# Reordering the first tile of a retention and maxout kernel: table load, decay tables, state steps, weight conversion and weight sums

## The chip, the cores and the metric

The kernel runs on one core of a Trainium2 chip. A core has a matrix engine (TensorE, PE in the profile, with its weight loads listed apart as PEld), a vector engine (VectorE, DVE), an activation engine (ScalarE, ACT), a general engine (GpSimd, POOL) and an engine that here only starts transfers (SyncE, SP). Each has its own queue of instructions and they wait for each other by semaphores. Data lies in a large on-chip memory (SBUF), and matrix products land in accumulators (PSUM). The metric is the time of one execution on the device, in microseconds (us), as the median of several runs.

## What is computed

Two steps follow each other. The first is a retention block (attention with a fixed decay in place of a softmax) over 8 batches, 8 heads, 576 positions and a head size of 64. The second is a feed-forward block: the larger of three products with three weight matrices, times a fourth.

```python
scores = scale * np.matmul(q, k.transpose(0, 1, 3, 2))
gamma = 1.0 - 2.0 ** (-5.0 - np.arange(H, dtype=np.float32))
Dmat = np.where(rel >= 0, gamma[:, None, None] ** rel[None, :, :], 0.0)   # rel: query minus key position
ret = scores * Dmat[None, :, :, :]
attn = np.matmul(ret, v).astype(np.float32)
x = attn.transpose(0, 2, 1, 3).reshape(B * S, H * D)                      # 4608 x 512
h = np.maximum(np.maximum(x @ w1, x @ w2), x @ w3)                        # 4608 x 768
return (h @ w_out).astype(np.float32)                                     # 4608 x 512
```

q, k and v are float32. The four weight matrices are float64 numbers, given to the kernel as 64-bit integers. The kernel makes float32 weights out of their bits.

## The kernel before

**Chunks and tiles.** The 4608 rows are cut into 36 chunks of 128 rows for retention and 9 tiles of 512 rows (four chunks) for the feed-forward block. While tile t goes through the feed-forward block, the chunks of tile t + 1 go through retention, step by step between the products; `steps` (L633) lists which step comes where. The chunks of tile 0 come first, alone, written out by hand at L603 to L631. There is no scheduler: every engine runs its instructions in the order in which the program text issues them.

**Retention of a chunk g.** `load(g)` (L151) starts the transfers of k, q and v, and the queue of SyncE also carries the weights. `decay_values` (L159) multiplies v by the key decay gk on GpSimd. `transposes` (L167) turns k and q on PE, and ScalarE copies the result out (L181). `scores` (L183) multiplies them on PE (L189), and VectorE masks the result into `st` (L192). `state` (L201) multiplies keys and decayed values (L208) into what is carried to the next chunk, and `keep` (L211) finishes it on VectorE (L216, or L218 and then GpSimd's L219) with the state decay gs. `values` (L227) makes the output: `st` times values (L241), and the carried state times q (L253); VectorE multiplies it by the output decay gq into `xT` (L260), the input of the feed-forward block. So the state of a chunk must be ready before the L253 products of the next.

**Conversion of the weights.** A piece is a block of 128 by 512 weights; there are 24: 18 of the three matrices and 6 of the fourth (`out`). `convert_all` (L418) is a generator that makes a piece in four steps, so that they can be laid between other work: `convert(n)` runs n steps. Of a piece, VectorE has five instructions: exponent bits (L428), fraction bits (L433), whole mantissa (L439), sign and exponent (L444) and the product (L450); ScalarE has three (L429, L431, L434). After a piece's product the load of the piece six further on is started (`load_weights(1)`), into one of the six buffers of the pool `wraw`.

**The feed-forward block of tile 0.** `ffn(0)` runs nine units of two products each. A unit (fp, i) covers matrix i and the blocks 2fp and 2fp + 1 of the hidden vector h. `up_plain` (L551) makes a product on PE in one of four accumulators, which are used in turn (two of the pool `ps_x`, two of `ps_y`). For the first matrix ScalarE copies it into h (L558), for the others VectorE takes the maximum (L557). Between the product and its maximum stands a call of `convert`, so that on VectorE the conversion steps lie ahead of the maximum in its queue. After the nine units `downs_plain` (L538) multiplies h with the fourth matrix: six rounds of four matmuls, into the same four accumulators (L543), so that the first four matmuls need the last four products out of these.

**Tiles 1 to 8** use Strassen's scheme (seven products of half size in place of eight; `up` and `downs`). For this the weights need sums and differences of their quarters: `weight_sums(n)` (L463) makes them for unit n with two instructions on VectorE (L471, L472) and two on GpSimd (L473, L474). Their tiles come from a pool `late`, which takes the memory of the conversion's buffers once `while_converting` is closed. Before, the first three units' sums come at the last three rounds of the down product, and the other six are put on a list of chores, which `up` works off at three places of each unit of tile 1 (`chore`), two in the first two places and none in the third. In `up`, the last product (product 3) adds to the accumulator x after VectorE has read it (L522).

**Transfers at the start.** ScalarE's queue starts the decay tables: gk (L100), gs (L599, two) and gq (L602, four). Its first copy (L181) is preceded by a load of the activation table; in the profile it stands between these transfers and the first copy.

Of the kernel before, what the change touches and what calls it, by code (L numbers as in the profile page):

```python
# [34 lines left out]
FP32 = mybir.dt.float32  # L35
# [16 lines left out]
def kernel(  # L52
# [14 lines left out]
    nc = tc.nc  # L67
    P = 128
# [3 lines left out]
    NP = H // 2  # L72
    NG = B * S // C
    NDC = DM // P
    NF = DF // P
# [22 lines left out]
    gq = const.tile([P, NP, C], FP32, name="gq")  # L98
    gs = const.tile([P, NP, D], FP32, name="gs")
    nc.scalar.dma_start(gk[:], key_decay)  # L100

    ident = const.tile([P, P], FP32, name="ident")
    make_identity(nc, ident[:])
# [47 lines left out]
    def load(g):  # L151
        if g >= BY_PE and ("q", g) not in raws:
            load_blocks(g, *range(C // 32))
        for n, src in (("k", k), ("q", q), ("v", v)) if g < BY_PE else (("k", k), ("v", v)):
            t = raws[n, g] = raw.tile([C, H, D], FP32, tag=n, name=n + "raw", bufs=4 if n == "k" else 3)
            for row, b, pos, m in spans(g):
                nc.sync.dma_start(t[row:row + m], src[b, :, pos:pos + m, :].rearrange("h p d -> p h d"))
# [37 lines left out]
    def begins(g):  # L195
        return g + 1 < NG and start_of(g + 1) != 0

    def half(j):
        return slice(D * j, D * (j + 1))

    def state(g):  # L201

        kr = raws["k", g]
        if begins(g):
            r = start_of(g) or 0
            kvs[g] = ps_r.tile([P, NP, D], FP32, tag="r", name="kv")
            for h in range(H):
                nc.tensor.matmul(kvs[g][half(h % 2), h // 2, :], lhsT=kr[r:, h, :], rhs=vds[g][r:, h, :],  # L208
                                 start=True, stop=True)

    def keep(g):  # L211
        if begins(g):
            kv = kvs.pop(g)
            t = states[g + 1] = stp.tile([P, NP, D], FP32, tag="state", name="state")
            if start_of(g) is not None:
                nc.vector.tensor_tensor(t[:], kv[:], gs[:], op=ALU.mult)  # L216
            else:
                nc.vector.tensor_tensor(t[:], kv[:], states[g][:], op=ALU.add)  # L218
                nc.gpsimd.tensor_tensor(t[:], t[:], gs[:], op=ALU.mult)  # L219
# [7 lines left out]
    def values(chunks, new_states=()):  # L227

        def before(g):
            return C if start_of(g) is None else start_of(g)

        t, i = divmod(chunks[0], CPT)
        pool, tag = (ps_r, "r") if chunks[0] >= CPT - 1 else (ps_y, "y")
        o = [pool.tile([P, len(chunks), NP // 2, C], FP32, tag=tag, name="o") for _ in range(2)]
        for m, g in enumerate(chunks):
            for n in range(NP):
                for c in range(2):
                    h = head(c, n)  # L240
                    nc.tensor.matmul(o[n % 2][half(c), m, n // 2, :], lhsT=vds[g][:, h, :],  # L241
                                     rhs=sts[g][:, h % 2, h // 2, :], start=m == 0 and n < 2,
                                     stop=before(g) == 0, skip_group_check=True)
        for g in new_states:
            state(g)
        for m, g in enumerate(chunks):
            old = before(g)
            if old > 0:
                for n in range(NP):
                    for c in range(2):  # L250
                        h = head(c, n)
                        r = half(h % 2)
                        nc.tensor.matmul(o[n % 2][half(c), m, n // 2, :old], lhsT=states[g][r, h // 2, :],  # L253
                                         rhs=qks[g]["q"][r, h // 2, :old], start=False, stop=True,
                                         skip_group_check=True)
        if i == 0:
            xT[t] = xpool.tile([P, NDC, NT], FP32, tag="xT", name="xT")
        for b in range(2):
            shape = [P, NP // 2, len(chunks), C]
            nc.vector.tensor_tensor(  # L260
                xT[t][:, b::2, i * C:(i + len(chunks)) * C].rearrange("p u (m c) -> p u m c", c=C),
                o[b][:].rearrange("p m u c -> p u m c"), gq[:, b::2, :].unsqueeze(2).to_broadcast(shape), op=ALU.mult)
        for g in new_states[:1]:
            keep(g)
        i += len(chunks) - 1
        if i == CPT - 1 and t > 0:
            x = xT[t]
            a11, a12, a21, a22 = (x[:, 2 * d:2 * d + 2, NH * r:NH * (r + 1)] for r in range(2) for d in range(2))
            s1, s2, s3, s4 = (spool.tile([P, 2, NH], FP32, tag=f"S{n}", name=f"S{n}") for n in (1, 2, 3, 4))
            nc.vector.tensor_tensor(s1[:], a21, a22, op=ALU.add)  # L270
            nc.vector.tensor_tensor(s2[:], s1[:], a11, op=ALU.subtract)
            nc.gpsimd.tensor_tensor(s3[:], a11, a21, op=ALU.subtract)
            nc.gpsimd.tensor_tensor(s4[:], a12, s2[:], op=ALU.subtract)
            xS[t] = {1: a11, 2: a12, 3: s4[:], 4: a22, 5: s1[:], 6: s2[:], 7: s3[:]}
# [4 lines left out]

    one = const.tile([P, 1], FP32, name="one")
    nc.vector.memset(one[:], 1.0)
    top = const.tile([P, 1], FP32, name="top")
    nc.vector.memset(top[:], 1151.0 * 2.0 ** 23)
    inf = const.tile([P, 1], FP32, name="inf")
# [176 lines left out]
    def weight_sums(n):  # L463
        if n >= len(units):
            return
        fp, i = units[n]
        half = [slice(0, DM // 2), slice(DM // 2, DM)]
        b11, b21 = (w_sb[i, 2 * fp][:, r] for r in half)
        b12, b22 = (w_sb[i, 2 * fp + 1][:, r] for r in half)
        t1, t2, t4 = (late["pool"].tile([P, DM // 2], FP32, name=f"T{m}_{i}_{fp}")[:] for m in (1, 2, 4))  # L470
        nc.vector.tensor_tensor(t1, b12, b11, op=ALU.subtract)  # L471
        nc.vector.tensor_tensor(t2, b22, t1, op=ALU.subtract)  # L472
        nc.gpsimd.tensor_tensor(b12, b22, b12, op=ALU.subtract)  # L473
        nc.gpsimd.tensor_tensor(t4, b21, t2, op=ALU.subtract)  # L474
        wT[fp, i] = {1: b11, 2: b21, 3: b22, 4: t4, 5: t1, 6: t2, 7: b12}
# [3 lines left out]
    def convert(n):  # L479
        for _ in range(n):  # L480
            next(converting, None)
# [78 lines left out]
    def ffn(t):  # L560

        h = hpool.tile([P, NF, NT], FP32, tag="h", name="h")
        for n, (fp, i) in enumerate(units):
            if t == 0:
                for fb in (2 * fp, 2 * fp + 1):
                    maximum = up_plain(t, h, fb, i)
                    convert(4)
                    maximum()
            else:
                if t == 1 and n == 0:  # L570
                    sums_of_outs()
                for _ in up(t, h, fp, i):
                    pass
                if i == 2:
                    sums_of_hidden(h, fp)
            yield
        if t == 0:
            convert(6)
            for fb, _ in enumerate(downs_plain(t, h)):
                convert(4 if fb < 2 else 4 * len(pieces))  # L580
                if fb in (1, 3):
                    yield
                if fb == 3:
                    while_converting.close()
                    late["pool"] = ctx.enter_context(tc.tile_pool(name="late", bufs=1))
                if fb > 2:
                    weight_sums(fb - 3)
            for n in range(3, len(units), 2):
                chores.extend([partial(weight_sums, n), partial(weight_sums, n + 1), lambda: None])
        else:  # L590
            chore(len(chores))
            for n, _ in enumerate(downs(t, h)):
                if n in (1, 3):
                    yield
        yield


    for j in range(2):
        nc.scalar.dma_start(gs[half(j)], state_decay[half(j), :, half(j)])  # L599
    for c in range(2):  # L600
        for b in range(2):
            nc.scalar.dma_start(gq[half(c), b::2, :], out_decay[half(b ^ c), NP // 2 * c:NP // 2 * (c + 1), :])  # L602
    warm(6)  # L603
    for g in range(CPT):
        load(g)
    load_weights(2)
    load(CPT)
    load_weights(4)
    decay_values(0)
    transposes(0)  # L610
    warm(2)
    scores(0)
    transposes(1)
    decay_values(1)
    values([0], [0])
    scores(1)
    transposes(2)
    decay_values(2)
    values([1], [1])
    transposes(3)  # L620
    decay_values(3)
    scores(2)
    convert(2)
    scores(3)
    convert(4)
    values([2], [2])
    decay_values(4)
    convert(2)
    values([3], [3])
    transposes(4)  # L630
    convert(2)  # L631

    def steps(t):  # L633

# [92 lines left out]
```

## Time and profile before

The time before is 799.95 us (median of 3 runs, 799.31 to 800.62); the profiled execution has a span of 797.8 us.

| stretch, us | what it holds | PE busy, us | DVE busy, us |
|---|---|---|---|
| 0 to 10 | first loads, chunk 0 | 6.84 | 0.30 |
| 10 to 20 | chunks 0 to 2 | 10.00 | 4.85 |
| 20 to 30 | chunks 2 and 3, first weights | 6.90 | 9.93 |
| 30 to 120 | tile 0, chunks 4 to 7 | 90.0 | 77.5 |
| 120 to 140 | end of tile 0, start of tile 1 | 18.70 | 17.79 |
| 140 to 700 | tiles 1 to 7 | 560.0 | 271.2 |
| 700 to 798 | tile 8 | 94.89 | 33.57 |

In the profile, the share of a stage is worth more than the share of the span: DVE is busy for 52% of the span but for 86% of the time from 30 to 120 us. A row of a timeline gives the start, the length, the engine, the line, the operation with its tiles and shapes, and in brackets the idle time ahead of it with what ended it. The table load of ScalarE takes 1.28 us and starts at 5.29; the first copy of kT starts at 6.58, that of qT at 7.07, and the first scores at 7.71. The first weight piece is waited for by ScalarE until 20.67. The nine units run from 30.16 to 103.9, the down product from 103.78 to 128, with retention between its rounds; conversion ends at 115.8. Weight sums run on VectorE and GpSimd from 124.4 to 149.5.

### The profile page before, as it was taken

The page shows a single profiled execution, that of the slowest core. Times are in us where ns is not written, and L with a number is a line of the kernel's source. Part 1 is how long each engine was busy: PE and PEld are TensorE (multiplying, and loading weights), DVE is VectorE, ACT ScalarE, POOL GpSimd, SP SyncE. Part 2 cuts the span into 40 slices and gives each one's busy share as a digit, 9 for nine tenths or more (in the row PEclk, how much of TensorE's full clock was granted, in tenths as well). Part 3 has the DMA queues.
Part 4 walks back from the last instruction along what each step waited for, and adds up shares of the span by engine and source line. Part 5 has one row for each costly group of instructions (what it writes and reads, how often), then busy time and mean ns, then how long its engine had stood idle before and what let it go on. Part 6 is the DMA issues. An engine that isn't in the chain of part 4 may idle for free.

```text
span 797.8 us, 13706 instructions
## 1 busy us (share of the span) xinstructions
PE 787.3 (99%) x5128; PEld 645.1 (81%) x5128; DVE 415.1 (52%) x833; ACT 174.0 (22%) x401; POOL 139.7 (18%) x158
## 2 busy tenths in 40 slices
PE   8899999999999999999999999999999999999998
PEld 7545546888888888888888888888888888888887
DVE  2897978664354634463535344543546344632341
ACT  2654642111111102111111111111111121112211
POOL 2110107421210130112211121112111201110000
PEclk9999999999999999999999999999999999999999
DMA  9985543333333332432233333333333323001001
GB/s 221 232 219 125 154 108 100 58 56 57 87 57 57 57 73 53 77 58 61 60 55 57 66 83 57 56 56 91 56 55 58 81 55 66 1 14 40 1 1 53
DMA packets 237506, 59.27 MB, mean 74 GB/s; under 512 B 218240, under 2 KB 236160, under 8 KB 237440
## 3 DMA queue, kind: packets, MB, share of 16 engines
q1 hardware_dynamic: 236176, 58.01, 33.2%
q8 instruction: 40, 0.66, 0.4%
q10 hardware_dynamic: 1264, 0.40, 0.2%
q14 instruction: 26, 0.21, 0.1%
HBM read 48.89 MB, written 9.44 MB: 73 GB/s over the span
## 4 chain that ended last, share of the span: by engine, by line
PE 96%; issue 1%; ACTq 1%; ACT 1%; DMA 0%; SPq 0%; POOL 0%; DVE 0%; DVEq 0%; POOLq 0%
PE x L492 31%; PE z L492 15%; PE dx L364 11%; PE up L554 8%; PE y L492 8%; PE dz L364 5%; PE s L189 4%; PE o L241 4%; PE dy L364 3%; PE down L543 2%; PE o L253 2%; PE kv L208 2%; PE kt L179 0%; PE qt L179 0%; ACTq L602 0%
## 5 line engine op out<-in xcount | busy, mean ns | idle before, releaser
L492 PE MATMUL x<-S,T 128*128 128x256 f32 x576 | 148.0, 379 | 0.2 <-ACT p L497 0.2
L492 PEld LDWEIGHTS x<-S,T 128*128 128x128 f32 x576 | 109.0, 190 | 16.0 <-ACT p L497 0.6
L342 POOL TENSOR_TENSOR H<-h 128x256 f32<-128x256 f32 x24 | 20.9, 872 | 320.8 <-DVE h L535 320.8
L492 PE MATMUL x<-xT,w 128*128 128x256 f32 x288 | 76.1, 387 | 0.0
L492 PE MATMUL x<-S,w 128*128 128x256 f32 x288 | 74.4, 381 | 1.1 <-DVE h L522 1.1
L492 PE MATMUL y<-xT,w 128*128 128x256 f32 x288 | 73.9, 379 | 0.0
L492 PE MATMUL z<-xT,T 128*128 128x256 f32 x288 | 73.9, 379 | 0.0
L492 PE MATMUL z<-S,w 128*128 128x256 f32 x288 | 73.9, 379 | 0.0
L522 DVE TENSOR_TENSOR tmp<-x,p 128x256 f32<-128x256 f32 x48 | 20.4, 425 | 100.0 <-PE x L492 100.0
L497 ACT COPY p<-x 128x256 f32<-128x256 f32 x72 | 26.8, 372 | 192.1 <-PE x L492 192.0
L260 DVE TENSOR_TENSOR xT<-o,gq 128x512 f32<-128x512 f32 (+1 forms) x40 | 23.6, 632 | 85.9 <-PE o L253 84.6
L554 PE MATMUL up<-xT,w 128*128 128x512 f32 x144 | 64.2, 601 | 0.0
L492 PEld LDWEIGHTS x<-S,w 128*128 128x128 f32 x288 | 49.3, 189 | 14.6 <-DVE h L522 1.5
L492 PEld LDWEIGHTS y<-xT,w 128*128 128x128 f32 x288 | 54.7, 190 | 7.4
L492 PEld LDWEIGHTS z<-S,w 128*128 128x128 f32 x288 | 54.7, 190 | 7.4
L492 PEld LDWEIGHTS x<-xT,w 128*128 128x128 f32 x288 | 53.0, 190 | 9.6 <-issue 1.5
L492 PEld LDWEIGHTS z<-xT,T 128*128 128x128 f32 x288 | 54.3, 189 | 7.9
L554 PEld LDWEIGHTS up<-xT,w 128*128 128x128 f32 x144 | 27.1, 193 | 32.2 <-issue 29.3
L219 POOL TENSOR_TENSOR state<-state,gs 128x256 f32<-128x256 f32 x24 | 19.8, 825 | 188.3 <-DVE state L218 188.3
L192 DVE TENSOR_TENSOR st<-s,causal 128x512 f32<-128x512 f32 x72 | 45.0, 684 | 13.8 <-PE s L189 12.9
L497 ACT COPY u<-x 128x256 f32<-128x256 f32 x72 | 26.8, 372 | 100.1 <-PE x L492 90.3
L161 POOL TENSOR_TENSOR vd<-vraw,gk 128x512 f32<-128x512 f32 x36 | 38.7, 1075 | 56.1 <-DMA vraw<-in_v_dram 56.1
(92 smaller groups left out, 1089.3 us busy)
## 6 DMA issues: line engine op xcount, KB each, us to landing
out_dram<-osb SPq DMA_DIRECT2D x35, 256.0 KB, 2.1
kraw<-in_k_dram SPq DMA_DIRECT2D x32, 256.0 KB, 3.0
vraw<-in_v_dram SPq DMA_DIRECT2D x32, 256.0 KB, 3.5
qraw<-in_q_dram SPq DMA_DIRECT2D x464, 16.0 KB, 1.8
kxraw<-in_k_dram SPq DMA_DIRECT2D x464, 16.0 KB, 1.8
bits<-in_moe_w_dram SPq DMA_DIRECT2D x18, 256.0 KB, 4.4
bits<-in_moe_w_dram SPq DMA_DIRECT2D x36, 128.0 KB, 4.1
bits<-in_moe_w_out_dram SPq DMA_DIRECT2D x6, 512.0 KB, 4.9
```

What stands on the lines that cost most here:

```text
L161: nc.gpsimd.tensor_tensor(t[:], raws.pop(("v", g))[:], gk[:].unsqueeze(2).to_broadcast([C, H, D]), op=ALU.mult)
L189: nc.tensor.matmul(s[j][:, p, :], lhsT=kT[r, p, :], rhs=qT[r, p, :], start=True, stop=True)
L192: nc.vector.tensor_tensor(st[:, j], s[j][:], masks[start_of(g)][:].unsqueeze(1).to_broadcast([C, NP, C]), op=ALU.mult)
L219: nc.gpsimd.tensor_tensor(t[:], t[:], gs[:], op=ALU.mult)
L241: nc.tensor.matmul(o[n % 2][half(c), m, n // 2, :], lhsT=vds[g][:, h, :], rhs=sts[g][:, h % 2, h // 2, :], start=m == 0 and n < 2, stop=be ...
L260: nc.vector.tensor_tensor(xT[t][:, b::2, i * C:(i + len(chunks)) * C].rearrange("p u (m c) -> p u m c", c=C), o[b][:].rearrange("p m u c - ...
L342: chores.append(lambda: (pool(s3, a11, a21, op=ALU.subtract), pool(s4, a12, s2, op=ALU.subtract)))
L364: nc.tensor.matmul(out[m], lhsT=hS[n](fp)[:, m * P:(m + 1) * P], rhs=late["T"][n][:, fp, :], start=first and fp == 0 and (m == 0 or last a ...
L492: nc.tensor.matmul(out[:], lhsT=w[:, d * P:(d + 1) * P], rhs=xS[t][n][:, d, :], start=first and d == 0, stop=d == 1, skip_group_check=True)
L497: nc.scalar.copy(c[:], src[:])
L522: nc.vector.tensor_tensor(c22, x[:], p7[:], op=ALU.add)
L554: nc.tensor.matmul(ps[:], lhsT=w_sb[i, fb][:, dc * P:(dc + 1) * P], rhs=xT[t][:, dc, :], start=(dc == 0), stop=(dc == NDC - 1))
```

## The change

It has five parts.

1. ScalarE copies one number (`first`) ahead of everything else, so that its table is loaded at the start and not in front of the first kT.
2. The state decay is loaded by SyncE behind the loads of chunk 1, and the output decay by ScalarE behind the copies of chunk 0's q and k, so that chunks 0 and 1 come ahead of them.
3. In the first four chunks the `state` and `keep` steps are called by themselves and earlier: `state` ahead of `values`, and `keep` ahead of the conversion steps that it stood behind. The call of `convert(4)` between `scores(3)` and the values is split and put behind.
4. In the last six of the nine units `convert` runs five steps a product in place of four, so that conversion is finished before the down product.
5. The sums of six units, not three, are then called in the six rounds of the down product, and the other three are spread over the chores one by one.

```diff
@@ tables
     nc.scalar.dma_start(gk[:], key_decay)
+    one = const.tile([P, 1], FP32, name="one")
+    nc.vector.memset(one[:], 1.0)
+    first = const.tile([P, 1], FP32, name="first")
+    nc.scalar.copy(first[:], one[:])
@@ state(g), keep(g)
         kr = raws["k", g]
+        kvs[g] = None
...
+        kv = kvs[g]
         if begins(g):
-            kv = kvs.pop(g)
@@ values
         for g in new_states:
-            state(g)
+            if g not in kvs:
+                state(g)
...
         for g in new_states[:1]:
-            keep(g)
+            if g >= CPT:
+                keep(g)
@@ ffn
                     maximum = up_plain(t, h, fb, i)
-                    convert(4)
+                    convert(4 if fp == 0 else 5)
                     maximum()
...
-            convert(6)
+            convert(4 * len(pieces))
+            while_converting.close()
+            late["pool"] = ctx.enter_context(tc.tile_pool(name="late", bufs=1))
             for fb, _ in enumerate(downs_plain(t, h)):
-                convert(4 if fb < 2 else 4 * len(pieces))
+                weight_sums(fb)
                 if fb in (1, 3):
                     yield
-                if fb == 3:
-                    while_converting.close()
-                    late["pool"] = ctx.enter_context(tc.tile_pool(name="late", bufs=1))
-                if fb > 2:
-                    weight_sums(fb - 3)
-            for n in range(3, len(units), 2):
-                chores.extend([partial(weight_sums, n), partial(weight_sums, n + 1), lambda: None])
+            for n in range(NF, len(units)):
+                chores.extend([partial(weight_sums, n), lambda: None, lambda: None])
@@ the first chunks
-    for j in range(2):
-        nc.scalar.dma_start(gs[half(j)], state_decay[half(j), :, half(j)])
-    for c in range(2):
-        for b in range(2):
-            nc.scalar.dma_start(gq[half(c), b::2, :], out_decay[half(b ^ c), NP // 2 * c:NP // 2 * (c + 1), :])
     for g in range(CPT):
         load(g)
+        if g == 1:
+            for j in range(2):
+                nc.sync.dma_start(gs[half(j)], state_decay[half(j), :, half(j)])
...
     transposes(0)
+    for c in range(2):
+        for b in range(2):
+            nc.scalar.dma_start(gq[half(c), b::2, :], out_decay[half(b ^ c), NP // 2 * c:NP // 2 * (c + 1), :])
     warm(2)
     scores(0)
     transposes(1)
     decay_values(1)
+    state(0)
     values([0], [0])
+    keep(0)
     scores(1)
     transposes(2)
     decay_values(2)
+    state(1)
+    keep(1)
     values([1], [1])
...
     scores(2)
     convert(2)
     scores(3)
+    state(2)
+    keep(2)
+    convert(2)
+    values([2], [2])
+    convert(2)
+    decay_values(4)
+    values([3], [3])
+    keep(3)
+    transposes(4)
     convert(4)
-    values([2], [2])
-    decay_values(4)
-    convert(2)
-    values([3], [3])
-    transposes(4)
-    convert(2)
```

More of the change, by code (lines that the diff above doesn't have):

```diff
@@ L274, in values @@
             xS[t] = {1: a11, 2: a12, 3: s4[:], 4: a22, 5: s1[:], 6: s2[:], 7: s3[:]}
-    one = const.tile([P, 1], FP32, name="one")
-    nc.vector.memset(one[:], 1.0)
     top = const.tile([P, 1], FP32, name="top")
```

## The prediction

> **What bounds the kernel now.** I read the busy shares first, then where TensorE (PE) waits, then the clock in those stretches, then VectorE's (DVE's) own order. The page's first line says that nothing but PE is near its limit over the whole span:
>
> ```profile
> PE 787.3 (99%) x5128; PEld 645.1 (81%) x5128; DVE 415.1 (52%) x833; ACT 174.0 (22%) x401; POOL 139.7 (18%) x158
> ```
>
> Only 10.5 us of 797.8 are idle on PE, so any gain must come from the few places where it waits. PE's timeline (start, length, idle before it and what ended that) names the two that matter here:
>
> ```profile
> 27.74 0.67 PE L253 MATMUL o<-qT,state 64*64 64x128 f32 x16 [3.01 <-POOL state L219]
> ...
> 30.16 7.87 PE L554 MATMUL up<-xT,w 128*128 128x512 f32 x16
> ...
> 134.88 1.13 PE L492 MATMUL x<-S,w 128*128 128x256 f32 x4 [1.08 <-DVE h L522]
> ```
>
> Windows of 3.41 us cut at the clock's steps (length; PE, PEld, DVE, ACT, POOL busy; granted clock) show what a wait costs beyond its length: where PE was busy for 0.56 of 3.41 us, and also for 1.69, the next 3.41 us ran at 0.50:
>
> ```profile
> 24.89:28.30 3.41, 0.56 (x16) 0.43 (x16) 3.38 (x8) 1.44 (x2) 1.72 (x2) 1.00 0.85 229
> 28.30:31.71 3.41, 3.41 (x14) 2.40 (x11) 3.41 (x6) 1.95 (x4) 1.67 (x2) 0.50 0.94 233
> 4.43:7.84 3.41, 1.69 (x14) 1.25 (x14) 0.00 (x0) 2.36 (x3) 0.68 (x1) 1.00 1.05 242
> 7.84:11.25 3.41, 3.41 (x24) 3.15 (x24) 1.29 (x2) 0.45 (x1) 0.50 (x2) 0.50 0.97 221
> ```
>
> DVE's timeline from 20 us on shows who holds the first product back: it works without a gap from 19.75 to 36 us, and xT of chunk 3, the last input of the first up product (L554 at 30.16), is at its end:
>
> ```profile
> 20.95 0.42 DVE L428 TENSOR_SCALAR expo<-bits 128x512 int32<-128x512 int32 x1
> ...
> 26.09 0.41 DVE L218 TENSOR_TENSOR state<-kv,state 128x256 f32<-128x256 f32 x1
> 26.42 0.68 DVE L439 SCALAR_TENSOR_TENSOR mant<-frac,mant 128x512 f32<-128x512 int32 x1
> 27.02 1.21 DVE L444 SCALAR_TENSOR_TENSOR expo<-bits,expo 128x512 int32<-128x512 int32 x1
> 28.27 1.42 DVE L450 TENSOR_TENSOR w<-mant,expo 128x512 f32<-128x512 f32 x1
> 29.60 0.74 DVE L260 TENSOR_TENSOR xT<-o,gq 128x256 f32<-128x256 f32 x2
> ```
>
> Last, DVE late in tile 0: xT of chunks 4 and 5 comes after a wait, the last maximum at 104.43, and between the two DVE has 0.28 us to spare out of 31.85:
>
> ```profile
> 73.26 1.29 DVE L260 TENSOR_TENSOR xT<-o,gq 128x512 f32<-128x512 f32 x2 [2.97 <-PE o L253]
> ...
> 104.43 0.68 DVE L557 TENSOR_TENSOR h<-h,up 128x512 f32<-128x512 f32 x1
> ...
> 73.26:105.11 31.85, 31.85 (x108) 15.38 (x109) 31.57 (x57) 17.31 (x27) 3.05 (x3) 1.00 0.63 170
> ```
>
> [...] in the timeline the maximum at 104.43 indeed stands behind conversion steps. [...] L444 and L450 took 1.21 and 1.42 us beside GpSimd's 26.58 to 29.13, 0.69 elsewhere.
>
> **The change, part by part.**
>
> *Table load and decay tables.* The load (1.28 us, from 5.29) leaves qT's path: qt ends at 5.98, so scores(0) can start near 6.2, not 7.71: 1.5 us earlier. 384 KB of tables leave the head of the transfers but are still sent before chunk 3. The transfers run at 200 to 280 GB/s from 2 us on, so chunk 3's q (landed 17.6) and the first weight piece (landed 20.6, which ScalarE's L429 waited for at 20.67) come about as before, 0.5 us earlier at best. ScalarE's FIFO now holds kT of chunk 1 behind four table issues (0.63 each, one waiting for chunk 1's v, near 9 us), and DVE's xT of chunk 0 waits for these tables until some 12.5 us, with state and scores(1) behind it. Both end before the 17.6 us of chunk 3's q. So I pay nothing for it and gain nothing by itself.
>
> *States ahead of weights.* DVE's order before xT of chunk 3 was: first piece, its second piece whole, states. In the built program after the change it is: two steps of piece one (0.67), scores 3 (1.20), state (0.33), the rest of piece one (1.93), xT of chunk 2 (0.67), two steps of piece two (0.67), xT of chunk 3 (0.67): 6.1, plus 0.5 where GpSimd's L219 collides (L433 took 0.95 at 30.93 beside it). From 20.65 that ends at 27.3; with the weights 0.5 earlier, 26.8. The 3.01 us wait goes (state at 22.85, L219 0.85, PE at 23.8). First up product: from 30.2 to 27.1 (the middle of 26.8 and 27.3), **3.1 earlier**. Its second half needs the second piece, which DVE now ends 3.5 later (state, three steps, two collisions), when PE gets there; the next unit needs pieces two and three at 34 to 36, and PE is there at 36. Its clock decides the rest. PE is idle for some 1.7 us before it, and 0.25 before qt of chunk 4. Before, this product lay partly in the cold window and lost 0.75 (7.8 against 7.0 to 7.1 later). Warm, it gains these: 3.9. Wholly cold it loses 1.7 against 0.75: 2.2. A window that holds both waits is 43% busy, under the 50% that was enough at 7.84, so cold is a little likelier; I take **2.6** for the step, ends 2.0 and 4.2.
>
> *Five steps a product.* A piece is four steps and 2.60 us of DVE (0.335+0.335+0.60+0.72+0.61, start to start). From xT of chunks 4 and 5 to the last maximum stand eight products. With eight more steps, ten pieces stand there and not eight: 5.2 us more on an engine with 0.28 to spare. The other work is the same (6 maxima of 0.60, 4 scores, 2 transposes, 2 states, xT, GpSimd collisions 1.85): 36.9 us and not 31.8. Queued behind the converted pieces is that maximum, and behind it PE: L543's fourth matmul uses the accumulator that the last up product filled. PE wants it at 103.88 + 3 × 0.86 = 106.45, that is 33.2 us after xT; before, the maximum ended at 105.11 and left 1.3 to spare. Now it ends 37.0 us after: a **stall of 3.8** (0.75 at the third matmul, the rest at the fourth). It doesn't depend on how early the stage begins: DVE reaches xT at about 67.5 and waits for PE there, as it did for 2.97. Such a gap leaves some window under 50% busy however it falls, so the clock halves for 3.41 us, of which 1.2 to 1.7 is lost: **1.5**. Ends for both together: 3.3 (no halving, collisions 0.5 less) and 6.5 (a collision of vd with DVE, 0.85, more).
>
> *Six sums in tile 0.* Four pairs (eight sums on DVE) now lie in the 5.3 us in which DVE waited for PE before 121.11, plus what ends conversion earlier; contended, 4 × 1.8 = 7.2, from about 108 to 115, so hidden. Between xT and the first h of tile 1, DVE has two pairs fewer, contended 1.4 to 1.8 each. L522, at 134.42, moves ahead of PE's need: the 1.08 wait goes. **1.1 gained**, ends 0 and 1.3.
>
> Sum: 2.6 − 3.8 − 1.5 + 1.1 = **1.6 slower**: 799.95 + 1.6 = 801.6.
>
> **Rivals.** *No change:* the first product starts warm (3.9), or the stall costs no clock. 3.9 − 3.8 − 1.5 + 1.1 = 0.3 slower; with no halving 1.2 faster: about 800. For it: half-busy windows[...]. Against: PE's 1.7 us gap at the first product. *Faster:* DVE's extra 5.2 us find slack and no maximum is waited for. Then 3.0 + 1.1 come through: 795.8. For it: DVE is 52% busy overall, waits 2.97 at 73.26, and conversion ended at 115.74, 5 us ahead of its use at 121. Against: none of this slack lies between xT and the last maximum. *Much slower:* cold first product (2.0), stall 4.6 with another collision, 1.7 of clock, 0.8 back: 3.5 slower, 803.5.
>
> **How the numbers follow.** Forecast 0.42, no change 0.31, faster 0.13, much slower 0.14. The forecast lies at the bound of 0.2% (1.6 us): 0.32 of it falls to slower, 0.10 to within. No change gives 0.29 within and 0.02 slower. So faster 0.13, same 0.39, slower 0.48. The range 798.8 to 803.6 leaves out the faster case and the outer part of the last.
>
> **What would show it.** Right: no wait at L253 near 24; first up product at 26.8 to 27.4; a wait of PE at the third and fourth matmul of the down product, ended by DVE's maximum, 3 to 4 us in all; a clock of 0.50 after it; no wait at the first tile-1 product 3. Wrong: DVE idle between xT of chunks 4, 5 and the last maximum, a down product that starts without a wait, or first weights landing well before 20.

## The result and the profile after

The changed kernel takes 809.48 us (median of 5 runs, 808.57 to 811.34) against 799.95: a ratio of 1.0117, interval 1.0098 to 1.0136, 9.5 us slower. The direction was forecast, the size was not (1.6; upper end of the range 803.6).

The page's first line says little again. PE's busy time rose by 2.9 us with the same number of instructions, and the span by 10.0 (807.8 against 797.8):

```profile
PE 790.2 (98%) x5128; PEld 645.0 (80%) x5128; DVE 413.2 (51%) x833; ACT 174.4 (22%) x402; POOL 139.8 (17%) x158
```

The down product and the first product of tile 1 on PE before, from the start of the one to the start of the other without a wait:

```profile
103.78 13.90 PE L543 MATMUL down<-w_out,h 128*128 128x512 f32 x32
...
127.98 1.03 PE L492 MATMUL x<-xT,w 128*128 128x256 f32 x4
```

PE's timeline after, at the places that the prediction showed (the kernel's lines are now 4 to 6 higher: L554 is L559, L557 is L562, L543 is L548, L492 is L497; a matmul of the down product is two in these rows, so that x4 is its first two, x2 the third and x26 what follows):

```profile
32.26 7.13 PE L559 MATMUL up<-xT,w 128*128 128x512 f32 x16 [1.08 <-ACT kT L185]
...
105.14 1.88 PE L548 MATMUL down<-w_out,h 128*128 128x512 f32 x4
111.89 1.89 PE L548 MATMUL down<-w_out,h 128*128 128x512 f32 x2 [4.87 <-DVE h L562]
115.43 13.15 PE L548 MATMUL down<-w_out,h 128*128 128x512 f32 x26 [1.65 <-DVE h L562]
138.88 1.03 PE L497 MATMUL x<-xT,w 128*128 128x256 f32 x4
...
144.62 1.08 PE L497 MATMUL x<-S,w 128*128 128x256 f32 x4
```

The 3.01 us wait for the state is gone, and so is the 1.08 us wait of tile 1. But the first up product starts at 32.26 instead of 30.16, and the down product has the forecast wait at its third and fourth matmul, at 6.52 us instead of 3.8. Summed along PE: the down product starts 1.36 later (105.14 against 103.78). From there to the first product of tile 1 it takes 33.74 us instead of 24.20, so 9.54 more: 6.52 of waits and 3.02 of slower matmuls. From that product to product 3 it takes 5.74 instead of 6.90, 1.16 less. 1.36 + 9.54 − 1.16 = 9.7: of the 10.0 us between the two traces (9.5 between the medians), all but 0.3 is placed.

The late start is not what the moved steps would do. ScalarE's first conversion instruction waits for the bits until 24.45, where it was 20.67 (the first line is before, the second after):

```profile
20.67 0.78 ACT L429 ACTIVATE mant<-bits,one 128x512 f32<-128x512 uint32 x1 [1.32 <-DMA bits<-in_moe_w_dram]
...
24.45 0.77 ACT L434 ACTIVATE mant<-bits,one 128x512 f32<-128x512 uint32 x1 [4.04 <-DMA bits<-in_moe_w_dram]
```

The windows from 10 to 20 us show the transfers themselves (last two columns: mean busy share of the DMA engines, a sum of the packets' times that can pass 1, and GB/s). First before:

```profile
10.00:20.00 10.00, 10.00 (x145) 8.80 (x145) 4.85 (x11) 3.32 (x6) 3.29 (x4) 0.94 1.04 252
```

and after:

```profile
10.00:20.00 10.00, 7.55 (x110) 5.93 (x108) 3.47 (x8) 2.92 (x6) 2.81 (x3) 1.00 1.34 211
```

The engines are busier and move less. From the packets of SyncE's queue in this window: before 7454 in 103.4% of 16 engines times 10 us, 22.2 ns each; after 6776 in 124.6%, 29.4 ns each. The weights pay for this all through tile 0: the page's transfer list has their landing times (median us from issue to landing, last column), two lines before and two after:

```profile
bits<-in_moe_w_dram SPq DMA_DIRECT2D x18, 256.0 KB, 4.4
bits<-in_moe_w_dram SPq DMA_DIRECT2D x36, 128.0 KB, 4.1
...
bits<-in_moe_w_dram SPq DMA_DIRECT2D x18, 256.0 KB, 5.5
bits<-in_moe_w_dram SPq DMA_DIRECT2D x36, 128.0 KB, 5.3
```

And DVE, which the forecast saw as the limit between xT of chunks 4 and 5 and the last maximum, now also waits for bits in that stretch:

```profile
88.62 0.43 DVE L433 TENSOR_SCALAR expo<-bits 128x512 int32<-128x512 int32 x1 [1.70 <-DMA bits<-in_moe_w_dram]
...
97.49 0.43 DVE L433 TENSOR_SCALAR expo<-bits 128x512 int32<-128x512 int32 x1 [2.34 <-DMA bits<-in_moe_w_out_dram]
...
114.69 0.68 DVE L562 TENSOR_TENSOR h<-h,up 128x512 f32<-128x512 f32 x1
```

### The profile page after: what moved, and what is told of

Same layout as the page of the kernel before. It is cut to its first block, busy times and chain, and to the rows that moved or that the text cites. A ratio compares the mean times of both kernels' runs of the same rounds, so it can differ in the third digit from the quotient of the medians.

```text
span 807.8 us, 13703 instructions
## 1 busy us (share of the span) xinstructions
PE 790.2 (98%) x5128; PEld 645.0 (80%) x5128; DVE 413.2 (51%) x833; ACT 174.4 (22%) x402; POOL 139.8 (17%) x158
## 5 line engine op out<-in xcount | busy, mean ns | idle before, releaser
L497 PE MATMUL x<-S,T 128*128 128x256 f32 x576 | 148.0, 379 | 0.4 <-ACT p L502 0.3
L497 PEld LDWEIGHTS x<-S,T 128*128 128x128 f32 x576 | 109.0, 190 | 16.3 <-ACT p L502 1.2
L497 PE MATMUL x<-xT,w 128*128 128x256 f32 x288 | 76.1, 387 | 0.0
L497 PE MATMUL x<-S,w 128*128 128x256 f32 x288 | 74.3, 381 | 0.0
L497 PE MATMUL z<-xT,T 128*128 128x256 f32 x288 | 73.9, 379 | 0.0
L497 PE MATMUL z<-S,w 128*128 128x256 f32 x288 | 73.9, 379 | 0.0
L497 PE MATMUL y<-xT,w 128*128 128x256 f32 x288 | 73.9, 379 | 0.0
L502 ACT COPY p<-x 128x256 f32<-128x256 f32 x72 | 26.8, 372 | 191.8 <-PE x L497 191.8
L559 PE MATMUL up<-xT,w 128*128 128x512 f32 x144 | 63.5, 596 | 1.1 <-ACT kT L185 1.1
L497 PEld LDWEIGHTS y<-xT,w 128*128 128x128 f32 x288 | 54.7, 190 | 7.4
L497 PEld LDWEIGHTS z<-S,w 128*128 128x128 f32 x288 | 54.7, 190 | 7.4
L497 PEld LDWEIGHTS x<-xT,w 128*128 128x128 f32 x288 | 53.0, 190 | 9.6 <-issue 1.5
L497 PEld LDWEIGHTS z<-xT,T 128*128 128x128 f32 x288 | 54.4, 189 | 7.8
L497 PEld LDWEIGHTS x<-S,w 128*128 128x128 f32 x288 | 49.3, 189 | 13.3 <-issue 1.5
L559 PEld LDWEIGHTS up<-xT,w 128*128 128x128 f32 x144 | 26.8, 190 | 32.9 <-issue 30.3
L502 ACT COPY u<-x 128x256 f32<-128x256 f32 x72 | 26.8, 372 | 99.7 <-PE x L497 90.1
```

The costliest lines, as they stand in the source:

```text
L497: nc.tensor.matmul(out[:], lhsT=w[:, d * P:(d + 1) * P], rhs=xS[t][n][:, d, :], start=first and d == 0, stop=d == 1, skip_group_check=True)
L502: nc.scalar.copy(c[:], src[:])
L559: nc.tensor.matmul(ps[:], lhsT=w_sb[i, fb][:, dc * P:(dc + 1) * P], rhs=xT[t][:, dc, :], start=(dc == 0), stop=(dc == NDC - 1))
```

## Experiments

"Part 1" to "part 5" are the parts listed under the change. Each ratio is to runs of the kernel before on the same chip, with its 95% interval in brackets. Differences in us are between medians, and the two need not agree to a tenth (for parts 1 and 3 below, 7.4 us by the medians and 8.5 by the ratio). A trace is of one execution, which can lie some us from its kernel's median; where that matters it is said.

### First: which part costs it

**Parts 4 and 5 alone.** The conversion and sums of the change on the kernel before:

```diff
-                    convert(4)
+                    convert(4 if fp == 0 else 5)
                     maximum()
...
-            convert(6)
+            convert(4 * len(pieces))
+            while_converting.close()
+            late["pool"] = ctx.enter_context(tc.tile_pool(name="late", bufs=1))
...
```

> The kernel before with parts 4 and 5 alone (five steps a product, six sums in the down product). Theory: two pieces more stand on VectorE ahead of the last maximum, so PE waits 3.5 to 4 us or more at the third and fourth matmul of the down product, the clock falls after it, and the wait at tile 1 goes: 3.5 to 6 us slower than before. Rival (the stall of the changed kernel came from its late weights only): no wait at the down product, about 1 us faster.

805.28 us, ratio 1.0069 (1.0053 to 1.0085), 5.6 slower. PE's timeline of this kernel has the stall at its forecast place:

```profile
106.77 1.13 PE L543 MATMUL down<-w_out,h 128*128 128x512 f32 x2 [1.05 <-DVE h L557]
110.33 14.08 PE L543 MATMUL down<-w_out,h 128*128 128x512 f32 x26 [2.44 <-DVE h L557]
```

3.49 us in all. The stretch on DVE, from xT at 73.31 to the end of the last maximum at 110.27, is 36.96 us; the forecast was 37.0. So the stall is the work of the five steps, and the transfers are not slowed here (242 GB/s at a share of 1.03 between 10 and 20 us).

**Part 2 alone.** The decay tables behind chunk 0:

```diff
-    for j in range(2):
-        nc.scalar.dma_start(gs[half(j)], state_decay[half(j), :, half(j)])
...
         load(g)
+        if g == 1:
+            for j in range(2):
+                nc.sync.dma_start(gs[half(j)], state_decay[half(j), :, half(j)])
```

> The kernel before with part 2 alone (decay tables behind chunks 0 and 1). Theory: the queue of SyncE is no longer held back at the start, the transfers run at about 217 GB/s and not at 240 to 280, the first weight piece lands near 24 and not 20.6, and the first up product starts 3 us late: 2.5 to 4 us slower. Rival (the order of the state steps or something else made the weights late): weights at 20.6 to 21, within 0.7 us of before.

800.76 us, ratio 1.0012 (1.0005 to 1.0020), 1.0 slower, and 254 GB/s at a share of 1.07. A small cost, but the tables do not slow the transfers: that theory fell.

**Parts 1 and 3** on the kernel before (the early copy, for which `one` moves up from further down, and the states' steps ahead):

```diff
+    one = const.tile([P, 1], FP32, name="one")
+    nc.vector.memset(one[:], 1.0)
+    first = const.tile([P, 1], FP32, name="first")
+    nc.scalar.copy(first[:], one[:])
...
+    state(0)
     values([0], [0])
+    keep(0)
```

> The kernel before with parts 1 and 3 alone (table load first, state steps ahead of weights). Theory: first weights at 20.6 as before, no wait of 3 us at L253, first up product at 27 to 28.5 (it may wait for kT of chunk 4, which stands behind the second piece on ScalarE): 1.5 to 3.5 us faster. Rival (the new order itself delays the start): 0 to 2 us slower.

A miss: 807.08 us, ratio 1.0106 (1.0076 to 1.0135), 7.4 slower where I expected a gain. Bits at 24.04, 213 GB/s at a share of 1.35.

**The change without parts 4 and 5:**

```diff
-                    convert(4 if fp == 0 else 5)
+                    convert(4)
```

> The changed kernel without parts 4 and 5. Theory: the late start stays (xT of chunks 4 and 5 at 74 to 75 and not 73.3), no wait at the down product, the wait of 1.1 us at tile 1 comes back: 1 to 2.5 us slower than before. Rival (the stall at the down product was a consequence of the late start): most of the 9.5 us stays.

A miss too: 808.59 us, ratio 1.0109 (1.0094 to 1.0124). Without the five steps there is no wait at the down product, and yet nearly all the loss remains; 213 GB/s at 1.34. Here PE waits 3.94 us at tile 1 for ScalarE's p, and in the kernel before this one 4.34.

These four and the changed kernel divide cleanly: slow transfers wherever part 1 is in (211 to 213 GB/s at shares of 1.34 and 1.35), fast ones wherever it is not (242 and 254 at 1.03 and 1.07). Part 1 has two sides: an instruction at the head of ScalarE, and a new tile. The pool `const` gives each small tile 32 bytes a partition, and all later tiles move up by that: in the built programs the first buffer of k starts at byte 70400 of its partition before, a multiple of 256, and at 70432 after; the first of the weight bits at 173824 and 173856.

### Second: the address or the instruction

**An unused tile of 4 bytes**, with no instruction added or moved:

```diff
     gs = const.tile([P, NP, D], FP32, name="gs")
+    pad = const.tile([P, 1], FP32, name="pad")
```

> The kernel before with one unused tile of 4 bytes per partition (the allocator gives it 32) put ahead of ident: no instruction is added or moved, but every later tile lies 32 bytes further on, as in the four kernels so far that have the early table load. Theory A (the shift of the transfers' destinations from a multiple of 64 bytes to 32 past one slows them): between 10 and 20 us about 213 GB/s with a busy share near 1.35, the first weight bits land at about 24 us instead of 20.7, and the time is 5 to 9 us over the kernel before. Theory T (the early table load itself, or the memset and copy in front of it, slows the transfers): no change, within 0.2%, 250 GB/s at a share near 1.05.

807.39 us, ratio 1.0084 (1.0061 to 1.0108). A tile that nobody reads or writes costs 7.3 us. Its window:

```profile
10.00:20.00 10.00, 9.37 (x117) 8.15 (x118) 3.25 (x8) 2.25 (x4) 2.09 (x2) 0.83 1.29 217
```

Theory A (the address) is shown. Theory T (the table load) is not needed for the loss, and the aligned kernel below, which keeps the early table load and has its fast transfers back (233 GB/s at a share of 0.98 between 10 and 20 us), refutes it.

**Unused tiles of 64 and of 128 bytes** (`[P, 16]` and `[P, 32]` in the same place):

> The same with an unused tile of 64 bytes, so that every later tile lies 64 bytes further on: the transfers' destinations are again multiples of 64, but no longer of 256. Theory A with a grain of 64 bytes: as the kernel before within 0.2%, about 250 GB/s at a share near 1.05. Theory A with a grain of 128 or 256 bytes: slow like the 32-byte shift. Theory T: no change.

> The kernel before with an unused tile of 128 bytes, so that every later tile lies 128 bytes further on (the destinations are multiples of 128, not of 256; a packet of q, k and v has 256 bytes). Grain of 128 bytes: as before within 0.2%, 250 GB/s at a share near 1.05. Grain of 256 bytes: 804 to 808 us, 217 GB/s at a share near 1.3, like the shifts of 32 and 64.

806.01 us, ratio 1.0085 (1.0064 to 1.0107), and 803.58 us, ratio 1.0034 (1.0016 to 1.0053). They move 218 and 219 GB/s at shares near 1.3, and ScalarE has its first bits at 23.93 and 23.86. So a multiple of 64 or of 128 is not enough, and the grain of 64 bytes that I allowed for is refuted; of the offsets tried, only multiples of 256 were fast. (128 bytes cost a little less than the 804 to 808 expected.) The times of the three shifts differ more than their transfers do. In the profiled executions, the wait at tile 1 for ScalarE's p was 4.54 us with 32 bytes, 1.48 with 64 and 1.03 with 128. It comes by another path. With 32 bytes:

```profile
136.77 1.07 ACT L548 COPY osb<-down 128x512 f32<-128x512 f32 x2 [5.96 <-DMA out_dram<-osb]
...
138.17 1.72 PE L493 MATMUL x<-S,T 128*128 128x256 f32 x4 [4.54 <-ACT p L498]
```

ScalarE's third copy of an output block into `osb`, which stands ahead of p in its queue, waits for the store of the first, whose block was ready at 129.95. In the trace of parts 1 and 3, with a like wait for p (4.34), SyncE issued the same store at 129.70, behind loads of k and v at 128.54 and 129.07, though the block was ready at 127.15. So the 4-byte tile's loss has two parts in this trace: the down product starts 3.77 later than before (107.55), and this wait is 4.32 longer (0.22 before). The third set of experiments comes back to the store.

**The changed kernel, aligned.** An unused tile of 224 bytes makes the shift 256 in all; nothing else differs from the changed kernel:

```diff
     gs = const.tile([P, NP, D], FP32, name="gs")
+    pad = const.tile([P, 56], FP32, name="pad")
```

> The changed kernel with an unused tile of 224 bytes ahead of the two small ones, so that its transfers' destinations lie 256 bytes further on than in the kernel before; nothing else differs from the changed kernel. Theory A: bits land at about 20.5 us, the first up product comes between 27 and 30 us, no bits wait over 0.5 us stands in the conversion's stretch, the waits for h at the down product come back to about 4 us, and the time is 801 to 804 us (799.7, plus the 5.5 that the five steps cost alone, less 2 to 3 of start). Theory T: 809 us as the changed kernel, bits at 24 us.

803.77 us, ratio 1.0046 (1.0031 to 1.0061): of 9.5 us, 5.7 were the address. Bits at 20.16, and PE's timeline:

```profile
27.96 7.13 PE L560 MATMUL up<-xT,w 128*128 128x512 f32 x16 [1.74 <-ACT kT L186]
...
105.02 1.88 PE L549 MATMUL down<-w_out,h 128*128 128x512 f32 x2 [2.29 <-DVE h L563]
108.55 13.16 PE L549 MATMUL down<-w_out,h 128*128 128x512 f32 x26 [1.65 <-DVE h L563]
```

The first product comes 2.2 earlier than before, and the wait at the down product is 3.94. One expectation missed in part: DVE still waits 1.59 for bits once. This execution took 802.32, the fastest of four.

**Parts 1 and 3, aligned** (the same pad on the combination that cost 7.4):

> The kernel before with the early table load and the states' steps ahead of the weights (the combination that cost 7.4 us), and the same 224-byte tile. Theory A: first up product between 27 and 30 us, no new wait for ScalarE's p at tile one, 796 to 798.5 us, faster than the kernel before. Theory T: 807 us, as without the tile.

798.47 us, ratio 0.9981 (0.9972 to 0.9990), 1.6 faster than before: a sign changed by a pad. Yet the profiled execution (800.31, slower than the median) shows none of the start left when xT of chunks 4 and 5 comes, at 73.25 (before: 73.26). The first up product started at 28.01, but PE had stood still for 3.02 us before it, waiting for ScalarE's copy of kT, and it ran 10.02 us instead of 7.87:

```profile
28.01 10.02 PE L560 MATMUL up<-xT,w 128*128 128x512 f32 x16 [3.02 <-ACT kT L186]
```

**Which transfers.** The destinations of q, k and v alone, or of the weight bits alone, 32 bytes past a multiple of 256, on the kernel before (in the second, the conversion's temporary tiles expo, mant and frac lie behind the bits and move with them):

```diff
+    raw.tile([P, 8], FP32, tag="pad", name="pad", bufs=1)
+    vpool.tile([P, 56], FP32, tag="padv", name="padv", bufs=1)
```

```diff
+    wraw.tile([P, 8], FP32, tag="pad", name="pad", bufs=1)
```

> The kernel before with the destinations of q, k and v alone 32 bytes past a multiple of 256, all the others at multiples of 256. If their packets of 256 bytes pay: slow transfers up to about 15 us (q and v of the last chunks 1 to 2 us later), the bits land at 22 to 24 us, and the time is 3 to 6 us over the kernel before. If only the bits pay: as before, within 0.2%.

> The kernel before with the destinations of the weight bits alone 32 bytes past a multiple of 256, q, k and v as before. If the bits pay: q, k and v come as before, the bits land 1 to 2 us later than 20.7, and the conversion waits for bits; 1 to 4 us over the kernel before. If only q, k and v pay: as before, within 0.2%.

802.76 us, ratio 1.0044 (1.0031 to 1.0057), and 801.16 us, ratio 1.0017 (1.0008 to 1.0026). The windows, of q, k and v shifted:

```profile
10.00:20.00 10.00, 9.32 (x116) 7.94 (x117) 3.16 (x8) 2.25 (x4) 2.09 (x2) 0.83 1.26 210
```

and of the bits shifted:

```profile
10.00:20.00 10.00, 9.91 (x152) 8.39 (x150) 5.00 (x11) 2.81 (x6) 3.82 (x4) 1.00 1.05 241
```

Both cost time, 3.1 and 1.5 us; q, k and v, whose rows are 256 bytes long in a head, cost more, and they alone slow the transfers of the start. In the first of these built programs every tile other than those of q, k and v starts where it did before, modulo 256 bytes, so it is these destinations that slow the transfers, and not the place of the other operands. How the bits' shift costs its 1.5 is not shown. Its expectation was met by the time and not by the trace (800.23, faster than the median):

```profile
20.32 0.80 ACT L430 ACTIVATE mant<-bits,one 128x512 f32<-128x512 uint32 x1 [2.10 <-DMA bits<-in_moe_w_dram]
...
130.93 1.13 PE L493 MATMUL x<-S,T 128*128 128x256 f32 x4 [1.69 <-ACT p L498]
```

The first bits are no later than before, DVE waits for bits for 0.9 us in all (before: not at all), and the largest new wait is the one for p. Together the two kernels account for 4.6 of the 7.3 us of the whole shift; the rest is not placed.

### Third: what is left, and where the start's gain goes

**Aligned, the last unit's maxima ahead of four of its five steps:**

```diff
-                    convert(4 if fp == 0 else 5)
+                    final = n == len(units) - 1
+                    convert(4 if fp == 0 else 1 if final else 5)
                     maximum()
+                    convert(4 if final else 0)
```

> The changed kernel with its destinations at multiples of 256, and in the last unit the maximum after one step of conversion instead of five, the other four behind it. Theory (what is left of the loss, 803.8 against 800, is the wait for h at the third and fourth matmul of down and the clock that it halves): both waits fall below 1 us, the down product comes near 14 us of run, and the time is 799 to 801 us. Rival (VectorE's conversion as a whole is the limit, so that the wait only moves to w_out at a later matmul): a wait of 3 us or more for w_out, 803 us.

800.07 us, ratio 0.9999 (0.9990 to 1.0009): 3.7 us gained over the aligned change, as the theory said. One wait of 1.25 us is left at the down product, a little over the 1 us expected, and the clock stays at 1.00 from 100 to 118.8 us:

```profile
29.58 8.83 PE L560 MATMUL up<-xT,w 128*128 128x512 f32 x16 [3.29 <-ACT kT L186]
...
104.16 2.74 PE L549 MATMUL down<-w_out,h 128*128 128x512 f32 x6
108.15 11.43 PE L549 MATMUL down<-w_out,h 128*128 128x512 f32 x26 [1.25 <-DVE h L563]
```

So the rest of the loss was VectorE's order in front of the last maxima and the clock behind it (in the aligned change 0.50 from 105.25 to 112.07), not the amount of conversion. This kernel has the same program as the aligned change up to the last unit of tile 0, and yet its trace has the first up product at 29.58 and not 27.96, and the down product at 104.16 and not 100.85. One trace does not tell what the earlier start is worth.

**Aligned, parts 1 and 3, kT of chunk 4 ahead of the third pair of steps:**

```diff
-    convert(2)
     decay_values(4)
     values([3], [3])
     keep(3)
     transposes(4)
-    convert(4)
+    convert(6)
```

> The aligned kernel with the early load and the states' steps (798.5), with the transposes of chunk 4 and the values of chunk 3 ahead of the third pair of conversion steps, so that the copies of kT do not stand behind piece two's steps on ScalarE. Theory (the first up product at 28.0 waits for that copy and then for nothing else): it starts at 25.5 to 27 us, and the time is 796 to 797.5 us. Rival (the second piece comes later by as much, or clock and later waits give it back): 798 to 799 us.

The first up product moved to 26.61 and xT of chunks 4 and 5 to 69.56, 3.7 ahead of before; but the time is 798.25 us, ratio 0.9975 (0.9963 to 0.9986), hardly better than without the move and short of the 796 to 797.5 expected. The runs spread from 796.02 to 801.51, and the trace is of a slow one (801.25); it says where the gain went there. ScalarE, SyncE (SPq) and PE at the end of tile 0:

```profile
121.90 0.59 ACT L553 COPY osb<-down 128x512 f32<-128x512 f32 x1 [11.88 <-PE down L549]
...
124.86 0.53 SPq L162 DMA_DIRECT2D vraw<-in_v_dram  x1
...
125.49 5.07 SPq L554 DMA_DIRECT2D out_dram<-osb  x4
128.99 1.22 ACT L553 COPY osb<-down 128x512 f32<-128x512 f32 x2 [5.64 <-DMA out_dram<-osb]
130.10 0.38 ACT L503 COPY p<-x 128x256 f32<-128x256 f32 x1
130.53 2.07 PE L498 MATMUL x<-S,T 128*128 128x256 f32 x4 [4.36 <-ACT p L503]
```

The output block is ready at 122.5, but its store is issued at 125.49, behind SyncE's loads for later chunks. The third copy into `osb` needs the first one's buffer back and waits 5.64 us, p stands behind it on ScalarE, and PE behind p.

**The same with the stores in ScalarE's queue:**

```diff
                     nc.scalar.copy(osb[:], b[:])
-                    nc.sync.dma_start(out[t * NT + m * P:t * NT + (m + 1) * P, :], osb[:])
+                    nc.scalar.dma_start(out[t * NT + m * P:t * NT + (m + 1) * P, :], osb[:])
```

> The aligned kernel with load, states and kT early (798.25), and the stores of tile zero's output issued by ScalarE instead of SyncE. Theory (the start's gain of 3.7 us is lost because the store waits in SyncE's queue behind the loads): the wait of 4.4 us for p at tile one falls below 1.5, and the time is 794 to 796 us. Rival (the store waits for the DMA engines, or the gain is lost again later): 798 us.

796.44 us, ratio 0.9960 (0.9946 to 0.9974): a little over the expected range, and the fastest of all. The five runs lie between 795.83 and 797.12, all below the median of the kernel without the move. In the trace the wait is 0.91:

```profile
122.74 0.36 ACTq L554 DMA_DIRECT2D out_dram<-osb  x1
...
127.30 1.13 PE L498 MATMUL x<-S,T 128*128 128x256 f32 x4 [0.91 <-ACT p L503]
```

**Everything mended** (parts 1, 3, 4, 5, aligned, kT early, maxima first), and then with the stores moved as well:

> Early load, states ahead, five steps, six sums, aligned destinations, kT ahead of the third pair of steps, and the maxima of the last unit ahead of four of its steps; the decay tables stay where they were before. If the causes add: 798.5 for load and states, 1 to 2 less for kT, 1.1 less for the wait of tile one, nothing for the down product: 795 to 797 us. Rival (the five steps cost elsewhere too): 799 us or more.

> The kernel with all parts mended (799.2), with the same move of the stores. Theory: the wait of 2.1 us for p goes, 796 to 797.5 us. Rival: 799 us.

Two misses: 799.16 us, ratio 0.9981 (0.9971 to 0.9992), and 800.69 us, ratio 1.0015 (1.0006 to 1.0025). In the second the wait for p fell as expected (2.13 to 1.14), but the wait for h at the down product rose from 1.49 to 3.73, with a slower product behind it (13.12 us for 26 matmuls, 11.43 in the first; the mean granted clock from 90 to 120 us was 0.94, and 1.00 in the first). Its DVE ran into the loads of the bits:

```profile
81.88 0.43 DVE L434 TENSOR_SCALAR expo<-bits 128x512 int32<-128x512 int32 x1 [1.59 <-DMA bits<-in_moe_w_dram]
90.20 0.43 DVE L434 TENSOR_SCALAR expo<-bits 128x512 int32<-128x512 int32 x1 [1.81 <-DMA bits<-in_moe_w_out_dram]
```

The first of these kernels waited there 0.97 in all, with the same conversion. So the causes do not simply add: at five steps a product the conversion comes close to its loads. Why the second waits more than the first is open, with no experiment on it; the two traces also lie 1.3 us below and 0.7 above the medians of their kernels.

## Why the forecast was wrong, step by step

**Table load and decay tables: the step that failed.** The prediction said that chunk 3's q and the first weight piece "come about as before, 0.5 us earlier at best". The first weight piece came 3.8 us later (24.45 and not 20.67), and PE turned chunk 3's q 1.1 later (19.07 and not 18.02). I had counted the instruction of part 1 and where its table load went, and not the 4-byte tile that came with it. Once aligned, the step holds: bits at 20.16. The price of moving the tables, put at nothing, is 1.0 by the experiment on part 2.

By what mechanism an address off a multiple of 256 bytes slows a transfer is not shown. The runs show what it cost: between 10 and 20 us a packet of SyncE's queue took 22.2 ns before, 29.4 in the changed kernel and 22.9 in the aligned one, and the shift of q, k and v, with rows of 256 bytes in a head, cost 3.1 us, that of the bits 1.5.

**States ahead.** The mechanism was right, and hidden. The wait for the state went. Aligned, xT of chunk 3 is done at 26.92, inside the forecast 26.8 to 27.3, but the first up product comes at 27.96 and not 27.1. It waits for ScalarE's copy of kT, which stands behind piece two's steps there, and which I did not see:

```profile
26.18 0.74 DVE L267 TENSOR_TENSOR xT<-o,gq 128x256 f32<-128x256 f32 x2
...
27.34 0.57 ACT L186 COPY kT<-kt 128x512 f32<-128x512 f32 x1
```

What the earlier start is worth to the next stage was forecast as 2.6, ends 2.0 and 4.2. It varies from execution to execution, with PE's wait for kT and the length of the product behind it: in the aligned change xT of chunks 4 and 5 comes 2.94 earlier than before (70.32; wait 1.74, first product 7.13 us long), with the maxima first 0.38 later (73.64; 3.29 and 8.83), with parts 1 and 3 alone at the same time as before (73.25; 3.02 and 10.02). By the medians, parts 1 and 3 are worth 1.6. And where four steps a product are kept, an earlier start meets a second limit, the store in SyncE's queue (with kT early, PE waited 4.36 us at tile 1 for p, which stood behind it).

**Five steps: the stall right, the clock mis-sized.** 3.8 was forecast; 3.49 with parts 4 and 5 alone, 3.94 in the aligned change. The 6.52 of the changed kernel is this stall plus what DVE lost to late bits in the stretch: 40.75 us (74.62 to 115.37) instead of 36.96, with 1.70 and 2.34 of waiting. The clock term was 1.5, for one halved window; what the product lost beyond its waits is 3.0 (9.54 less 6.52; aligned 3.02, alone 3.17). By an estimate from the kernel with the maxima first, some 0.5 of this is not the clock: with one wait and no halved clock, that kernel lost 0.26 beyond its wait, and here there are two waits. That leaves about 2.5 for the clock. Windows of 3.41 us of the changed kernel, cut at the clock's steps, show why:

```profile
108.74:112.13 3.39, 0.24 (x1) 0.24 (x2) 3.35 (x8) 0.82 (x2) 0.00 (x0) 1.00 0.23 35
112.13:115.54 3.41, 1.76 (x3) 0.19 (x2) 3.38 (x8) 2.61 (x4) 0.00 (x0) 0.50 0.24 39
115.54:118.95 3.41, 3.41 (x4) 1.40 (x5) 3.31 (x6) 0.00 (x0) 1.11 (x2) 0.50 0.85 168
118.95:122.36 3.41, 3.41 (x9) 1.52 (x8) 3.34 (x5) 0.00 (x0) 3.41 (x4) 1.00 0.23 34
```

A second window followed at half clock: the first halved one, with the wait for the fourth matmul in it, was itself only half busy (1.76 of 3.41), and the next 3.41 us ran at 0.50 again. The aligned change has the same pair of windows (105.25 to 112.07, the first with 1.76 us busy). The prediction had read from the trace of before that a window with 1.69 us of 3.41 busy was followed by a halved one, and applied it once.

**Six sums.** 1.1 gained was forecast, 1.16 measured.

With the sizes of the aligned change, the sum is −2.93 + 3.94 + 3.02 − 1.21 = 2.8 between the two traces (3.7 by the medians), where the forecast had −2.6 + 3.8 + 1.5 − 1.1 = 1.6. That the first term agrees so well is luck, as its spread shows. The rest is the address: 5.7 by the medians, and 6.9 between these two traces, 4.29 of it the later start of the down product and 2.58 the longer stall.

## What to carry to other kernels

A new tile is part of a change even when nothing uses it: look where it puts the destinations of the transfers behind it, and try them at multiples of 256 bytes, the only offsets that were fast here (pad, or allocate small tiles last): ScalarE had its first bits at 18.9 to 21.1 us with those of q, k, v and the bits there, and at 23.6 to 24.7 with all of these 32, 64 or 128 bytes further on. Before a start gain is counted, follow it to the first thing that does not move with it; here that was a store in a queue of loads. A stall cost the clock twice here: its first halved window was only half busy (1.76 of 3.41 us), and a second one followed. And set a trace's time beside the median of its kernel's runs before a start that it shows is counted as gained.

## What the runs showed that I had not expected

- Destinations 32, 64 or 128 bytes past a multiple of 256 took the loaded transfers from 252 GB/s to 217 to 219, with a higher busy share (1.04 to about 1.3). Over the whole run, with 73 GB/s in the mean, it showed less: in the changed kernel k's median landing went from 3.0 to 3.3 us and v's from 3.5 to 3.9, and the 16 KB blocks of q stayed at 1.8.
- An unused tile of 4 bytes moved this kernel by 7.3 us, more than parts 4 and 5 of the change together (5.6).
- Two halved clock windows in a row (112.13 to 118.95) from one pair of waits, about 2.5 us lost.
- A store that stands behind loads in SyncE's queue held PE for 4.4 us, and in ScalarE's queue for 0.9 (4.36 and 0.91 in the two traces; 798.25 and 796.44 by the medians).
